# Transform mixing with a squared-ReLU layer on one core: the order of VectorE's sums, its side work and ScalarE's side work inside a step

## The chip, the core and the metric

The kernel runs on one core of a Trainium2 chip. PE is TensorE (matmuls; PEld its weight loads), DVE VectorE, ACT ScalarE, POOL GpSimd, and SP the engine that issues most DMAs. Every engine works its own instructions strictly in the order in which the program lists them, and waits on semaphores for the others. SBUF is the on-chip memory, PSUM the accumulators into which PE writes, in banks. The metric is the device time of one execution in microseconds (us); every time below is in us.

## The reference

```python
X = np.fft.fft(x, axis=1); X = np.fft.fft(X, axis=2)   # x: (8, 3008, 256) float32
a = X.real.reshape(8 * 3008, 256)
h = a @ w_in                                           # w_in: (256, 2048)
r = np.maximum(h, 0.0)
out = (r * r) @ w_out                                  # w_out: (2048, 256)
```

Eight batches, each a real part of a two-dimensional Fourier transform, then two matrix products with a squared ReLU between them, all in float32.

## The kernel before

**Blocks and steps.** A batch has 1506 columns (the transform's symmetry gives the rest), cut into six blocks of 252 columns (`CK`; the last has 246). The 2048 hidden features are 16 chunks of 128, taken in pairs, so a block has `NJ` = 8 steps, and the program 384, numbered `i`. "Step 2" below means i modulo 8 = 2. The loop at the end of the function lists one step's instructions for all engines; since each engine keeps that order, the place of a call in the loop is its place in the engine's queue.

A step's *front* (`front`, L928 to L935): four PE products of 252 columns, two into the bank hP and two into hQ; then DVE's *split*: two operations on hP (L932, tile `he`) and two on hQ (L934, L935), each writing one half of the hidden tile g and, mirrored, the other. Then ACT's relu (L939) and square (L942) on g, and POOL's sums of thirds of g (`sums_even`, L955 to L957, in even steps, `sums_odd`, L965 to L972, in odd ones) into a tile s.

Behind the front, in the same step, PE runs the *back* of an earlier pair of steps: the second matrix product, as a fast product of small matrices with 20 instead of 24 block products. In odd steps `first_half` runs 12 products from g and s into the banks F0, F1, F2, in even steps `second_half` 8 products from s into S0, S1, S2 (L990; each bank holds three slots of 168 columns). Their weights are sums of parts of w_out, kept in `wsum` (12 of them) and in place, which `sum_wout` (L379) makes on DVE beside steps 8 to 14 of batch 0.

**The gather.** After four pairs a block's banks are full. `gather` returns five functions that bring them together in the tile c: `early` (two ACT copies out of F1 and F2, L1045 and L1046), `upper` (two DVE operations that read F0, L1049 and L1050), `lower` (an ACT copy out of S0 and six DVE operations, L1053 to L1059, that read S0, S1, S2), `joins` (L1062 to L1065; L1064 still reads S0) and `rest` (L1068 to L1070). A block's last first half falls into step 1 of the next block, `early` at its end; `upper` into step 2, `lower` behind that step's second half, `joins` into step 3, `rest` into step 4. `store` (DVE transposes at L1105 and L1107, eight DMAs from SP) follows for the two mirror halves in steps 5 and 6; in the last block it goes over PE transposes (L1089). The next block's first half needs the F banks in step 3, its second half the S banks in step 4.

**The next batch's transform.** `ahead(b + 1)` is a list of pieces, each a planned time and a function, that prepare the next batch beside the steps of this one. First come DVE's folds of the eight tiles of x (`fold`: fs at L520, fd at L524, which also issues the load three tiles ahead, sc at L536, dc at L540, w at L550, a shuffle at L560) and rotations between them (butterflies at L573 and L574, turns at L596 and L625); pieces of planned time 0.0 between these are ACT's (copies and scalings, L583 to L631, tables L410 to L417). For batch 1 there are also small pieces for one separate column (L464 to L494) and four transform groups for it. Last come eight transform groups (`even` and `odd`, the functions in the set `beside`): eight small PE products each into a bank `pd`, ACT copies (L688, L766, L791) and DVE joins (L711 to L717, L799 to L819). The pool `psh` has two banks in turn for hP, hQ and pd, so a group takes hP's bank once the split has read it, and the next step's hQ takes pd's once the joins have read that.

`SHARE` and `pace` spread the planned times over a batch's steps: each step may spend pace x share. `pieces_beside(False)` runs right behind the front and lists pieces while the budget and a step's room (1.9, in batch 0 2.4) last, those of time 0.0 at once. `pieces_beside(True)` is called by `run` before the fourth product of a half (the hook) and lists a transform group.

The order in a step is: front, pieces, then `upper`, `joins` or `rest` when due (`pending`), then `store` when due, the first or second half with its hook, `lower`, relu, square, POOL's sums, `early`.

Of the kernel before, what the change touches and what calls it, by code (L numbers as in the profile page):

```python
# [9 lines left out]
F32 = mybir.dt.float32  # L10
# [5 lines left out]
P = 128  # L16
# [68 lines left out]
def kernel(  # L85
# [12 lines left out]
    nc = tc.nc  # L98
# [7 lines left out]
    NJ = NFC // 2  # L106
# [29 lines left out]
    tt = nc.vector.tensor_tensor  # L136
    act = nc.scalar.activation
# [235 lines left out]
    def place(to):  # L373
        return wsum[:, to] if isinstance(to, int) else to

    def sum_wout(qs, which):

        u, v, op, to = SUMS[which]
        tt(out=place(to)[:, qs], in0=u[:, qs], in1=v[:, qs], op=op)  # L379
# [568 lines left out]
    gt = nc.gpsimd.tensor_tensor  # L948
# [45 lines left out]
    def first_half(q, n, gA, gB, s, hook=None):  # L994

        if q == 0:
            open_banks(("F0", "F1", "F2"))
        a, b = thirds(gA, n), thirds(gB, n)
        r1, r3, r0, r2 = ([v[:, h] for v in w] for w in (a, b) for h in range(2))
        run((("F0", 2, 0, r2[2]), ("F0", 1, 1, r2[1]), ("F0", 1, 2, s[:, 9]), ("F0", 0, (1, 2), r2[0]),  # L1000
             ("F0", 0, 3, s[:, 0]), ("F1", 2, (1, 1), r1[2]), ("F2", 1, (0, 0), r0[0]), ("F2", 1, 9, s[:, 1]),
             ("F2", 0, (0, 3), r3[2]), ("F1", 0, 6, r0[2]), ("F1", 1, 5, r3[1]), ("F1", 1, 4, s[:, 11])), q, n, hook)

    def second_half(q, n, s, hook=None):

        if q == 0:
            open_banks(("S0", "S1", "S2"))
        run((("S0", 0, 8, s[:, 2]), ("S0", 1, (0, 1), s[:, 4]), ("S0", 2, (0, 2), s[:, 8]), ("S1", 0, (1, 0), s[:, 6]),
             ("S1", 1, 11, s[:, 10]), ("S1", 2, 10, s[:, 3]), ("S2", 0, 7, s[:, 7]), ("S2", 1, (1, 3), s[:, 5])),
            q, n, hook)  # L1010
# [21 lines left out]
    def gather(n):  # L1032
# [3 lines left out]
        cf = ep.tile([P, 5, TB], F32, name="cf", tag="cf")[:, :, 0:tb]  # L1036
        cs = ep.tile([P, 2, TB], F32, name="cs", tag="cs")[:, :, 0:tb]
        vt = ep.tile([P, 7, TB], F32, name="vt", tag="vt")[:, :, 0:tb]
# [3 lines left out]
        u4 = cf[:, 4]  # L1042

        def early():
            nc.scalar.copy(cf[:, 2:5], F1)  # L1045
            nc.scalar.copy(cf[:, 0:2], F2[:, 0:2])  # L1046

        def upper():
            tt(out=o1[0], in0=F0[:, 0], in1=u4, op=SUB)  # L1049
            tt(out=pair(1, 1), in0=F0[:, 1:3], in1=cf[:, 4:5].to_broadcast([P, 2, tb]), op=ADD)  # L1050

        def lower():
            nc.scalar.copy(cs, S0[:, 0:2])  # L1053
            tt(out=o1[0], in0=o1[0], in1=S0[:, 0], op=SUB)
            tt(out=o1[2], in0=o1[2], in1=S0[:, 2], op=ADD)
            tt(out=cf[:, 3], in0=cf[:, 3], in1=S0[:, 1], op=SUB)
            tt(out=vt[:, 0:2], in0=S1[:, 0:2], in1=cs, op=ADD)
            tt(out=vt[:, 3:5], in0=S2[:, 0:2], in1=vt[:, 0:2], op=ADD)
            tt(out=vt[:, 2], in0=S1[:, 2], in1=vt[:, 4], op=ADD)  # L1059

        def joins():
            tt(out=vt[:, 5:7], in0=cf[:, 0:3:2], in1=vt[:, 2:4], op=ADD)  # L1062
            tt(out=o0[2], in0=vt[:, 6], in1=vt[:, 5], op=SUB)
            tt(out=o0[2], in0=o0[2], in1=S0[:, 2], op=ADD)  # L1064
            tt(out=pair(0, 0), in0=cf[:, 1:4:2], in1=vt[:, 5:7], op=ADD)  # L1065

        def rest():
            tt(out=pair(1, 1), in0=pair(1, 1), in1=vt[:, 0:4:3], op=ADD)  # L1068
            tt(out=pair(1, 1), in0=pair(1, 1), in1=vt[:, 1:3], op=SUB)  # L1069
            tt(out=o1[0], in0=o1[0], in1=vt[:, 4], op=ADD)  # L1070
# [202 lines left out]
    SHARE = (1.2, 1.2, 0.6, 0.0, 0.6, 0.8, 0.8, 1.2)  # L1273

    def share(i):
        return 0.0 if i < PLAIN + 2 else SHARE[i % NJ]

    def pieces_beside(at_hook):


        nonlocal spent
        room = 1.9 if i >= per else 2.4
        while side:
            t, f = side[0]
            if f in beside:
                if at_hook and spent + t / 2 <= 0:
                    side.pop(0)
                    f()
                    spent += t
                return  # L1290
            if t and (at_hook or t > room or spent + t / 2 > 0):
                return
            side.pop(0)
            f()
            spent, room = spent + t, room - t

# [113 lines left out]
    i = 0  # L1410
# [4 lines left out]
    for i in range(PLAIN, len(steps) + 7):  # L1415
# [15 lines left out]
        hook = None  # L1431
        if PLAIN <= i < len(steps):
            spent -= pace * share(i)
            pieces_beside(False)
            hook = (3, lambda: pieces_beside(True))
        while pending and pending[0][0] <= i:
            pending.pop(0)[1]()
        while finished and finished[0][0] <= i:
            store(*finished.pop(0)[1:])
        group = (i - 3) // 2  # L1440
# [4 lines left out]
        elif at >= NJ and at < len(steps):  # L1445
            b_, k0_, n_, j_ = steps[at]
            q = j_ // 2
            if not last_half:
                first_half(q, n_, made["g", at], made["g", at + 1], made["s", group], hook)
                if q == NJ // 2 - 1:  # L1450
                    c_, ops = gather(n_)
                    gather_next = ops[0]
                    final = at + 2 == len(steps)
                    pending += [(i + 1, ops[1]), (i + 2, ops[3]), (i + 3, ops[4])]
                    lower = (i + 1, ops[2])
                    finished += [(i + 3 + final * k + (not final) * (1 + k), b_, k0_, n_, s_, c_, final)
# [9 lines left out]
        if gather_next:  # L1466
            gather_next()

# [62 lines left out]
```

## Time and profile before

| what | value |
|---|---|
| median of 3 runs | 1994.09 us (1993.31 to 1999.09) |
| profiled execution | 1996.1 us |
| its span, first to last instruction | 1994.3 us |
| mean granted TensorE clock | 0.988 |
| busy: PE, DVE, POOL, ACT | 1899.8, 1722.7, 1564.0, 966.6 us |
| DVE waits for PE's hP (he L932) | 149.8 us in 101 waits |
| POOL waits for ACT (s L965 behind g L942) | 261.9 us in 150 waits |
| PE waits for DVE's second upper operation (F behind c L1050) | 17.7 us in 12 waits |

The profile is one execution. A row of a group gives the line, the engine, output and inputs, and the mean duration; a row of waits gives the waiting instruction, what it waited for, the total, the number of times and the longest. Rows of the timeline are start, length, engine, line and tiles, with the wait in brackets. Rows of stretches give the busy time of each engine between two times and the clock that TensorE was granted (1.00 is full). Neighbouring DVE rows overlap a little, so a row's duration is somewhat more than an instruction's share of DVE's time.

### The profile page before, as it was taken

The numbers are of one execution on the slowest core, as the hardware profiler recorded it, in microseconds if no ns is written. First come the engines' busy times: TensorE is split into PE (matmuls) and PEld (weight loads), VectorE is DVE, ScalarE is ACT, GpSimd is POOL, SyncE is SP. The second block draws the span as 40 slices with busy tenths as digits, with TensorE's granted clock in tenths as the row PEclk, the third lists the DMA queues.
The fourth block names the chain that finished last, engine by engine and source line by source line (L and its number), as shares of the span: only waits on it lengthen the run. The fifth ranks groups of instructions, "written<-read, shape, count | busy, mean of one in ns | idle before, by whom it ended". The sixth has DMA issues, their size and how long they took to land. (4 is left out here: it accounts for less than half of the span.)

```text
span 1994.3 us, 33439 instructions
## 1 busy us (share of the span) xinstructions
PE 1899.8 (95%) x11408; PEld 1765.2 (89%) x11408; DVE 1722.7 (86%) x3462; ACT 966.6 (48%) x1274; POOL 1564.0 (78%) x2111
## 2 busy tenths in 40 slices
PE   9989889999999989999999999999999999999998
PEld 7678889898898989989898998989989998999997
DVE  8798988999889998999879998899978999766765
ACT  5744444455444454445444544445544455444443
POOL 3477767898788877888778887788877888688886
PEclk9998999999999999999999999999999999999999
DMA  6331101111011101111101120111101110010010
GB/s 196 101 42 22 46 14 30 38 42 22 14 39 41 37 16 22 40 37 34 23 22 29 38 43 14 22 37 40 33 14 30 40 25 14 14 25 16 14 24 22
DMA packets 151306, 68.43 MB, mean 34 GB/s; under 512 B 131143, under 2 KB 142881, under 8 KB 151136
## 3 DMA queue, kind: packets, MB, share of 16 engines
q1 hardware_dynamic: 150590, 65.74, 15.0%
q8 instruction: 91, 1.49, 0.3%
q14 instruction: 79, 0.65, 0.1%
q0 software_dynamic: 416, 0.43, 0.1%
q10 hardware_dynamic: 130, 0.12, 0.0%
HBM read 41.54 MB, written 24.69 MB: 33 GB/s over the span
## 5 line engine op out<-in xcount | busy, mean ns | idle before, releaser
L939 ACT ACTIVATE g<-g 128x1008 f32<-128x1008 f32 (+1 forms) x384 | 399.8, 1041 | 684.6 <-DVE g L935 541.1
L932 DVE SCALAR_TENSOR_TENSOR he<-ew,gE,hP 128x252 f32<-128x252 f32 (+1 forms) x748 | 317.4, 464 | 150.9 <-PE hP L928 149.8
L928 PE MATMUL hQ<-Qt,G 128*128 128x252 f32 (+3 forms) x1496 | 385.3, 380 | 36.2 <-DVE dc L717 13.4
L942 ACT ACTIVATE g<-g 128x1008 f32<-128x1008 f32 (+1 forms) x384 | 399.4, 1040 | 12.0
L928 PE MATMUL hP<-Pt,G 128*128 128x252 f32 (+1 forms) x1496 | 379.3, 376 | 6.7 <-DVE he L932 6.7
L928 PEld LDWEIGHTS hQ<-Qt,G 128*128 128x128 f32 (+1 forms) x1496 | 277.3, 190 | 92.4 <-PE hP L928 28.5
L990 PE MATMUL F<-s,wsum 128*128 128x168 f32 (+1 forms) x1504 | 343.1, 310 | 0.0
L965 POOL TENSOR_TENSOR s<-g 128x168 f32<-128x168 f32 (+1 forms) x188 | 105.8, 563 | 268.3 <-ACT g L942 261.9
L990 PE MATMUL F<-g,wout 128*128 128x168 f32 (+1 forms) x1504 | 314.5, 312 | 0.0
L990 PE MATMUL F<-g,wsum 128*128 128x168 f32 (+1 forms) x1504 | 280.8, 310 | 17.7 <-DVE c L1050 17.7
L934 DVE TENSOR_TENSOR g<-he,hQ 128x504 f32<-128x504 f32 (+1 forms) x374 | 253.4, 678 | 49.9 <-DVE he L932 4.4
L928 PEld LDWEIGHTS hP<-Pt,G 128*128 128x128 f32 x1496 | 265.7, 190 | 26.8 <-DVE he L932 9.5
L990 PE MATMUL S<-s,wout 128*128 128x168 f32 (+1 forms) x1504 | 282.3, 306 | 0.1
L990 PE MATMUL S<-s,wsum 128*128 128x168 f32 (+1 forms) x1504 | 277.0, 307 | 4.7 <-DVE c L1064 3.3
L990 PEld LDWEIGHTS F<-g,wsum 128*128 128x128 f32 x1504 | 243.6, 193 | 30.9 <-issue 17.0
L990 PEld LDWEIGHTS S<-s,wsum 128*128 128x128 f32 x1504 | 238.1, 190 | 20.1 <-POOL s L957 5.4
L990 PEld LDWEIGHTS F<-s,wsum 128*128 128x128 f32 x1504 | 255.6, 194 | 0.0
L935 DVE TENSOR_TENSOR g<-he,hQ 128x504 f32<-128x504 f32 (+1 forms) x374 | 250.5, 670 | 0.0
L990 PEld LDWEIGHTS F<-g,wout 128*128 128x128 f32 x1504 | 247.7, 195 | 0.5 <-issue 0.5
L990 PEld LDWEIGHTS S<-s,wout 128*128 128x128 f32 x1504 | 232.2, 190 | 0.7 <-POOL s L972 0.4
L968 POOL TENSOR_TENSOR s<-s 128x336 f32<-128x336 f32 (+1 forms) x188 | 184.0, 979 | 14.7
L955 POOL TENSOR_TENSOR s<-g 128x336 f32<-128x336 f32 (+1 forms) x188 | 174.6, 929 | 23.4 <-ACT g L942 18.8
(210 smaller groups left out, 2720.1 us busy)
## 6 DMA issues: line engine op xcount, KB each, us to landing
out_dram<-os SPq DMA_DIRECT2D x376, 56.0 KB
xt<-in_x_dram SPq DMA_DIRECT2D x39, 384.0 KB
xt<-in_x_dram SPq DMA_DIRECT2D x63, 128.0 KB
ew<-e_dram SPq DMA_DIRECT2D x39, 126.0 KB
out_dram<-os SPq DMA_DIRECT2D x288, 7.0 KB
raw<-in_moe_w_in_dram SPq DMA_DIRECT2D x16, 256.0 KB
raw<-in_moe_w_out_dram SPq DMA_DIRECT2D x16, 256.0 KB
xt<-in_x_dram SPq DMA_DIRECT2D x2, 512.0 KB
```

The lines of the kernel that those rows point to most:

```text
L928: nc.tensor.matmul(to[:, h, 0:n], w[:, fs], v[:, ks], start=h == 0, stop=True, skip_group_check=True)
L932: nc.vector.scalar_tensor_tensor(out=t[:, h, 0:n], in0=window[b, k0][:, 0:n], scalar=gE[:, fc:fc + 1], in1=hP[:, h, 0:n], op0=ALU.mult, op ...
L934: tt(out=g[:, :, 0:n], in0=t[:, :, 0:n], in1=hQ[:, :, 0:n], op=ALU.add)
L935: tt(out=g[:, :, n:2 * n][:, :, ::-1], in0=t[:, :, 0:n], in1=hQ[:, :, 0:n], op=ALU.subtract)
L939: act(g[:, :, 0:2 * n], g[:, :, 0:2 * n], AF.Relu)
L942: act(g[:, :, 0:2 * n], g[:, :, 0:2 * n], AF.Square)
L955: gt(out=s[:, 0:2], in0=a0, in1=a2, op=ADD)
L965: gt(out=s[:, 11], in0=b2[:, 0], in1=b1[:, 0], op=SUB)
L968: gt(out=s[:, 4:6], in0=s[:, 4:6], in1=s[:, 10:11].to_broadcast([P, 2, tb]), op=SUB)
L990: nc.tensor.matmul(acc[nm][:, slot, 0:tb], w, v, start=q == 0 and nm not in begun, stop=q == NJ // 2 - 1, skip_group_check=True)
```

## The change

- `gather`: `early` copies three slots instead of five. `upper` has three more DVE operations that read F1 and F2 from PSUM and form the upper results in c. `lower` adds S0's third slot to both halves at once, so that nothing behind it reads S0. `joins` is three operations and `rest` three of 168 columns, without PSUM. `rest` is listed in step 5; in the last block it goes to POOL, inside `lower`.
- The order in a step: front, `pending`, `store`, then the pieces, then the half. The pieces of time 0.0 are no longer listed among the others but at the end of the step (`free_pieces`), behind relu, square, POOL's sums and `early`; a piece of 0.0 at the head of the list ends a step's pieces.
- `SHARE` has 0.0 in steps 2 and 3 and 1.6 in steps 1 and 7; batch 0 has shares of its own (`FIRST`) and a room of 3.0. The hook stands before the third product.
- `store` falls into steps 6 and 8 (step 0 of the block after).
- In `first_half` two slots of F1 change places, in `second_half` S1's third product comes last.
- Six of the 32 weight sums go to POOL (three in each of steps 8 and 9).

```diff
     def sum_wout(qs, which):
-        tt(out=place(to)[:, qs], in0=u[:, qs], in1=v[:, qs], op=op)
+        (gt if which % 2 and qs.start == 0 and which < 12 else tt)(out=place(to)[:, qs], in0=u[:, qs], in1=v[:, qs], op=op)
...
-             ("S1", 1, 11, s[:, 10]), ("S1", 2, 10, s[:, 3]), ("S2", 0, 7, s[:, 7]), ("S2", 1, (1, 3), s[:, 5])),
+             ("S1", 1, 11, s[:, 10]), ("S2", 0, 7, s[:, 7]), ("S2", 1, (1, 3), s[:, 5]), ("S1", 2, 10, s[:, 3])),
...
         def early():
-            nc.scalar.copy(cf[:, 2:5], F1)
-            nc.scalar.copy(cf[:, 0:2], F2[:, 0:2])
+            nc.scalar.copy(cf[:, 1:3], F1[:, 0:2])
+            nc.scalar.copy(cf[:, 0], F2[:, 0])
 
         def upper():
-            tt(out=o1[0], in0=F0[:, 0], in1=u4, op=SUB)
-            tt(out=pair(1, 1), in0=F0[:, 1:3], in1=cf[:, 4:5].to_broadcast([P, 2, tb]), op=ADD)
+            tt(out=o1[0], in0=F0[:, 0], in1=cf[:, 2], op=SUB)
+            tt(out=pair(1, 1), in0=F0[:, 1:3], in1=wide(cf[:, 2:3]), op=ADD)
+            tt(out=o0[1], in0=F1[:, 2], in1=cf[:, 1], op=ADD)
+            tt(out=o0[2], in0=F1[:, 0], in1=cf[:, 0], op=SUB)
+            tt(out=o0[0], in0=F2[:, 1], in1=cf[:, 0], op=ADD)
 
         def lower():
             nc.scalar.copy(cs, S0[:, 0:2])
             tt(out=o1[0], in0=o1[0], in1=S0[:, 0], op=SUB)
-            tt(out=o1[2], in0=o1[2], in1=S0[:, 2], op=ADD)
-            tt(out=cf[:, 3], in0=cf[:, 3], in1=S0[:, 1], op=SUB)
+            tt(out=o0[1], in0=o0[1], in1=S0[:, 1], op=SUB)
+            tt(out=both, in0=both, in1=wide(S0[:, 2:3]), op=ADD)
             tt(out=vt[:, 0:2], in0=S1[:, 0:2], in1=cs, op=ADD)
             tt(out=vt[:, 3:5], in0=S2[:, 0:2], in1=vt[:, 0:2], op=ADD)
-            tt(out=vt[:, 2], in0=S1[:, 2], in1=vt[:, 4], op=ADD)
+            if final:
+                rest()
+            tt(out=v13, in0=S1[:, 2], in1=v14, op=ADD)
 
         def joins():
-            tt(out=vt[:, 5:7], in0=cf[:, 0:3:2], in1=vt[:, 2:4], op=ADD)
-            tt(out=o0[2], in0=vt[:, 6], in1=vt[:, 5], op=SUB)
-            tt(out=o0[2], in0=o0[2], in1=S0[:, 2], op=ADD)
-            tt(out=pair(0, 0), in0=cf[:, 1:4:2], in1=vt[:, 5:7], op=ADD)
+            tt(out=pair(0, 0), in0=pair(0, 0), in1=vt[:, 2:4], op=ADD)
+            tt(out=v13, in0=v8, in1=v13, op=SUB)
+            tt(out=both, in0=both, in1=wide(vt[:, 2:3]), op=ADD)
 
         def rest():
-            tt(out=pair(1, 1), in0=pair(1, 1), in1=vt[:, 0:4:3], op=ADD)
-            tt(out=pair(1, 1), in0=pair(1, 1), in1=vt[:, 1:3], op=SUB)
-            tt(out=o1[0], in0=o1[0], in1=vt[:, 4], op=ADD)
+            late(out=v9, in0=v9, in1=v15, op=SUB)
+            late(out=o1[1], in0=o1[1], in1=v9, op=ADD)
+            late(out=o1[0], in0=o1[0], in1=v14, op=ADD)
...
-    SHARE = (1.2, 1.2, 0.6, 0.0, 0.6, 0.8, 0.8, 1.2)
+    SHARE = (0.5, 1.6, 0.0, 0.0, 0.5, 0.6, 0.5, 1.6)
+    FIRST = (1.2, 1.6, 0.3, 0.5, 1.0, 1.0, 1.0, 1.6)
 
     def share(i):
-        return 0.0 if i < PLAIN + 2 else SHARE[i % NJ]
+        return 0.0 if i < PLAIN + 2 else FIRST[i % NJ] if i < per else SHARE[i % NJ]
+
+    def free_pieces():
+        while side and not side[0][0]:
+            side.pop(0)[1]()
+
+    def pieces():
+        nonlocal spent
+        room = 1.9 if i >= per else 3.0
+        while side:
+            t, f = side[0]
+            if f in beside or not t or t > room or spent + t / 2 > 0:
+                return
+            side.pop(0)
+            f()
+            spent, room = spent + t, room - t
+
+    def piece_beside():
+        nonlocal spent
+        if side and side[0][1] in beside and spent + side[0][0] / 2 <= 0:
+            t, f = side.pop(0)
+            f()
+            spent += t
...
-        hook = None
-        if PLAIN <= i < len(steps):
-            spent -= pace * share(i)
-            pieces_beside(False)
-            hook = (3, lambda: pieces_beside(True))
         while pending and pending[0][0] <= i:
             pending.pop(0)[1]()
         while finished and finished[0][0] <= i:
             store(*finished.pop(0)[1:])
+        hook = None
+        if i < len(steps) and share(i):
+            spent -= pace * share(i)
+            pieces()
+            hook = (2, piece_beside)
...
-                    pending += [(i + 1, ops[1]), (i + 2, ops[3]), (i + 3, ops[4])]
+                    pending += [(i + 1, ops[1]), (i + 2, ops[3])] + ([] if final else [(i + 4, ops[4])])
...
         if gather_next:
             gather_next()
+        free_pieces()
```

## The prediction

> **What bounds the kernel now.** I read the busy totals first, then the granted clock, then one batch cut into its six blocks beside two blocks of the last batch, which has no transform to prepare, then PE's waits in batches 1 to 6, then the instructions around two of these waits. "Step 2" is the step whose number modulo 8 is 2; a block has steps 0 to 7.
>
> ```profile
> PE 1899.8 (95%) x11408; PEld 1765.2 (89%) x11408; DVE 1722.7 (86%) x3462; ACT 966.6 (48%) x1274; POOL 1564.0 (78%) x2111
> ```
> ```profile
> core 0: 1994.3 us, clock 0.988
> ```
> ```profile
> 559.50:596.11 36.61, 36.57 (x227) 34.58 (x226) 34.21 (x64) 16.53 (x19) 31.12 (x42) 1.00 0.13 34
> 596.11:635.88 39.77, 37.63 (x226) 34.37 (x225) 38.55 (x69) 19.02 (x23) 33.18 (x45) 1.00 0.17 39
> 635.88:674.35 38.47, 37.44 (x227) 34.50 (x226) 37.08 (x72) 19.49 (x25) 34.66 (x46) 1.00 0.16 38
> 674.35:712.86 38.51, 37.38 (x226) 34.66 (x225) 36.85 (x68) 19.27 (x24) 33.46 (x44) 1.00 0.17 38
> 712.86:757.68 44.82, 40.46 (x258) 38.38 (x257) 39.29 (x84) 22.86 (x34) 33.85 (x48) 1.00 0.12 21
> 757.68:798.37 40.69, 39.65 (x258) 38.13 (x257) 31.09 (x69) 18.00 (x24) 30.71 (x44) 1.00 0.08 14
> ...
> 1798.10:1834.50 36.40, 36.40 (x226) 34.96 (x226) 24.85 (x51) 17.94 (x20) 30.89 (x46) 1.00 0.10 19
> ```
> ```profile
> PE hQ L928 <- DVE dc L717: 13.4, 6, 2.2
> PE F L990 <- DVE c L1050: 12.9, 10, 2.0
> PE hQ L928 <- DVE Pt L717: 10.5, 6, 2.1
> PE pd L787 <- DVE he L932: 6.2, 6, 1.0
> ```
> ```profile
> 609.90 1.62 DVE L596 SCALAR_TENSOR_TENSOR w<-w,turn,f 94x257 f32<-94x257 f32 x2
> 611.45 1.38 DVE L520 TENSOR_TENSOR fs<-xt 96x512 f32<-96x512 f32 x1
> 612.75 0.32 DVE L1049 TENSOR_TENSOR c<-F,cf 128x168 f32<-128x168 f32 x1
> 612.99 0.49 DVE L1050 TENSOR_TENSOR c<-F,cf 128x336 f32<-128x336 f32 x1
> 613.63 0.81 PE L990 MATMUL F<-g,wsum 128*128 128x168 f32 x4 [2.00 <-DVE c L1050]
> ```
> ```profile
> 727.30 1.01 DVE L574 TENSOR_TENSOR w<-f,w 94x257 f32<-94x257 f32 x1
> 728.25 0.32 DVE L1049 TENSOR_TENSOR c<-F,cf 128x168 f32<-128x168 f32 x1
> 729.61 0.34 DVE L717 TENSOR_TENSOR dc<-db,pd 128x188 f32<-128x188 f32 x1
> 730.10 1.09 PE L928 MATMUL hQ<-Qt,G 128*128 128x252 f32 x4 [2.24 <-DVE dc L717]
> ```
>
> In the stretches the columns are length, then busy time of PE, PEld, DVE, ACT, POOL. In the last batch a block is pure PE: 36.40 of 36.40, with DVE at 24.85. A block of 246 columns is then 36.4 x 246/252 = 35.5, and a transform group costs PE 0.87 (eight records from 724.52 to 725.39), so a batch with eight groups can't be under 5 x 36.4 + 35.5 + 7.0 = 224.5. Batch 2 takes 238.9, 14.4 over: 0.2, 3.4, 2.1, 2.1, 4.9, 1.7 by block. In blocks 1 to 3 DVE is busy 37 to 38.6, more than PE's 36.4, so DVE sets them. In block 4 it is order: pieces stand ahead of the sums that free F (the wait at 613.63) and of the joins that free a transform's bank, which the next hQ takes (730.10).
>
> **Counting DVE's lateness.** A split takes DVE 2.15 back to back and unhindered ends 3.06 after its front starts. Steps are 5.12 (odd) and 3.98 (even). The next hQ starts 0.85 into the next step, so PE waits once a split is late by more than 2.9 (odd) or 1.8 (even). Lateness grows by 2.15 plus other DVE work less the step. Costs are mean rows less the 0.08 by which neighbours overlap: fs 1.0, fd 0.93, sc 0.72, dc 0.68, w 1.5 (two of 0.82), a shuffle 0.64, a butterfly 1.6, a pair of turns 1.36. For the old order, with its waits for F and for transform banks, this gives 0, 1.7, 2.4, 1.2, 5.2, 0.9 by block: 11.4 against the trace's 14.4, short mainly in block 1.
>
> **The change, part by part.**
>
> *The sums.* Old: upper 0.65, lower 2.1, joins 1.74, rest 2.3 = 6.8. New: upper has three more reads of PSUM at 0.24 (the spacing of L1054 to L1056) = 1.37; lower trades a 168-wide for a 336-wide one, +0.17 = 2.27; joins of two 336- and one 168-wide operations 1.65; rest of three 168-wide ones on SBUF, 0.36 (shortest L1063) to 0.73 each (mean L1070), taken at 0.57 = 1.7. That is 7.0: DVE's load doesn't fall. ACT's two copies lose 0.2. F's first two operations come where they came, F1 and F2 are used five products (1.43) later, so the longer upper is hidden there.
>
> *Pieces behind the sums, new shares.* I wrote the pieces out by plan: their sum is 48.6 per batch, and the pace rises from 1.34 to 1.64 a share. Steps 2 and 3 get none. For example block 2 has fd, sc, dc in step 0, w and shuffle in 1, fs and fd in 4, sc, butterfly, dc in 5 (behind rest: 4.7 in all), w in 6, turns and shuffle in 7. Its lateness runs 2.4, 3.0, 2.1, 3.6, 1.6, 1.7, 3.4, 2.1, and the waits past 2.9 and 1.8 sum to 3.3. In the same way the blocks give 0, 0.6, 3.3, 2.4, 3.0, 0.9 = 10.2. Of block 4's 3.0, 2.4 is new: the first transform group stands in step 5 behind step 4's two last butterflies (3.2), its bank is hP's, and hP is freed 2.4 late for a group that now stands behind two products, 0.29 earlier than behind three. Differences to the old count: -1.1, +0.9, +1.2, -2.2 in blocks 1 to 4, -1.2 together; and the wait for F, counted at 1.2, is 2.0 in the trace and leaves whole, so I take -2.3 a batch, -14 for six. Ends: -43, if the four waits above go (13.4 + 12.9 + 10.5 + 6.2) and nothing follows; +13, if those come back and blocks 2 and 3 lose their 2.1.
>
> *The clock.* The mean grant of 0.988 costs 0.012 x 1994 = 24. It drops for 3.4 at a time, 1.7 lost, seven times in batches 1 to 6 (0.64 granted from 1700.5 to 1705.2, behind a 2.11 idle), always behind idle of 2.0 or more, though not behind each. Three such idles per batch become one: -8 of 12; ends -12 and 0. The Trainium skill (TensorE: Matmul & The Clock Gate, Part 1) has the clock fall after a whole idle window of about 3.4 us. The trace disagrees: 2.0 us were enough. By that page this term would be nothing and the time 8 us longer.
>
> *Batch 0.* Four steps hold 22.5 over their floor of 5.12 (and 0.87 for a group): 10.10 at 145.7, 13.22 at 169.0, 9.65 at 239.3, 11.79 at 264.0. At 169.0 the table copies and the first group share a step, with DVE 2.3 late; the new plan has the copies at that step's end and the group a step later: -5.7. At 264.0 the last butterflies still stand ahead of the joins, but hP's 3.8 wait goes: -3.3. At the other two, pieces still follow: -1 and -1.3. The wait for S behind L1064 (2.2, once) goes, as lower frees S: -1.5. Sum -12.8; ends -18 and -5.
>
> *Six weight sums to POOL.* Alone they are 0.34 apart on DVE (three in 1.09 at 90.35), with POOL busy 0.76 is common and 1.12 the longest. Between -2 (six gone) and +2 (the other six stretched to the longest, two taken off): 0, as POOL waits there (4.55 before 92.73) and PE waits for DVE by no more than 0.4 before 111. The Trainium skill (SBUF — State Buffer, Who interferes with whom) says that a DVE instruction with two SBUF inputs and a GpSimd instruction that reads SBUF exclude each other. By that rule six pairs follow one another, 6 x (0.34 + some 0.7, between POOL's 0.54 for 168 and 0.89 for 336) = 6.2 for the old 4.1, and the sum would be 2 higher.
>
> *At nothing.* ACT's pieces behind the squares: PE's waits for POOL are 1.1 in six batches though POOL waits 185.8 for ACT, and the next relu waits for a split behind the pieces anyway; uncovered, POOL's sums come late to the S products, up to the 1.6 of one turn. Stores move from steps 5 and 6 to 6 and 8, ahead of the pieces: eight issues of some 0.4 on SP now stand before a step's xt load, which leads by three tiles; DVE waited 2.5 for xt once, at the start. The load of POOL in the blocks is unchanged. The order of products within F and S changes no count.
>
> *The end.* Rest leaves DVE for POOL there, but upper is 0.7 longer ahead of lower, with PE's 4.0 wait behind it all: -0.5 (-1.5 to +0.5).
>
> Sum: -14 - 8 - 12.8 - 0.5 = -35. The profiled execution took 1996.1 (span 1994.3 and 1.8 around), 2.0 over the median of the runs: 1996.1 - 35 - 2 = **1959**.
>
> **The rivals.** (1) The waits go and little returns, since collisions with POOL thin out: -43 - 12 - 18 - 1 = -74, 1920, or half way, 1938. For: blocks 0 and 5 have DVE room (34.2 and 31.1). Against: 1 to 3 have none. (2) The order changes but DVE's bound holds: the waits of blocks 1 and 4 return as late splits, +13, against -12.8 in batch 0: 1994, no change. For: DVE's 38.55 in a 39.77 block. Against: block 4's waits are order, not load. (3) Slower: pieces bunched behind odd steps collide with POOL. L550 takes 0.34 to 1.17 by where POOL stands; squares that come earlier keep POOL busy through more pieces. Priced by the count, pieces 10% dearer bring 15.6 a batch against the old 11.4, +25, and no clock gain: 1994 + 25 - 13 = 2006. It decides from about 5%. For: DVE rows with two SBUF inputs scatter, those with PSUM don't. Against: three rests of 168 replace 336s. By the Trainium skill's rule above, whichever starts second stands for the other's whole instruction.
>
> **How the numbers follow.** Forecast 0.64 (own range 1940 to 1980, from -2.3 a batch give or take 3); rival 1 0.14, rival 2 0.09, rival 3 0.13. Faster by over 0.3%, about what the measurement can tell: 0.64 + 0.14 = 0.78; same 0.09; slower 0.13. The range of 1932 to 1994 leaves out rival 3 and the lower part of rival 1.
>
> **What would show it.** Right: no PE wait for upper in F, nor of some 2 for a transform's joins in hQ; blocks 1 to 5 of a batch near 38, 39.4, 39.7, 41.7 and 41.5 (one group moves from block 4 to 5); the step at 169 under 9; a grant above 0.99. Wrong: DVE busy over 38 in each of blocks 1 to 3, longer L550 and L520 rows, PE waiting for he at the group of step 5 by more than 2.4, or for POOL in S.

## The result and the profile after

The changed kernel takes 1966.59 us (median of 4 runs, 1963.47 to 1970.06) beside 1993.7 for the kernel before (4 runs): ratio 0.9859, 95% interval 0.9834 to 0.9883, so 1.4% faster. The forecast was 1959, 1.8% faster. The profiled execution took 1965.07, 1.5 under the median.

The page's busy totals and the granted clock, after:

```profile
PE 1889.9 (96%) x11408; PEld 1764.7 (90%) x11408; DVE 1719.0 (88%) x3547; ACT 958.9 (49%) x1274; POOL 1549.7 (79%) x2120
```
```profile
core 0: 1963.3 us, clock 0.991
```

Batch 2 of the changed kernel, cut into its six blocks (length, then busy time of PE, PEld, DVE, ACT, POOL):

```profile
550.68:587.61 36.93, 36.55 (x227) 34.71 (x226) 33.94 (x65) 16.18 (x18) 31.88 (x43) 1.00 0.15 39
587.61:625.51 37.90, 37.14 (x226) 34.75 (x225) 36.74 (x69) 19.14 (x24) 32.42 (x45) 1.00 0.11 28
625.51:665.55 40.04, 37.63 (x227) 34.66 (x226) 38.84 (x74) 19.38 (x25) 33.71 (x46) 1.00 0.17 47
665.55:704.62 39.07, 37.15 (x227) 34.81 (x226) 37.88 (x72) 19.25 (x25) 32.97 (x44) 1.00 0.13 36
704.62:745.76 41.14, 39.35 (x251) 37.58 (x250) 36.38 (x83) 22.30 (x33) 31.28 (x45) 1.00 0.08 18
745.76:786.23 40.47, 40.47 (x267) 39.12 (x265) 33.05 (x75) 17.95 (x25) 31.21 (x44) 1.00 0.07 17
```

PE's waits in batches 1 to 6 (total, times, longest), after:

```profile
PE hP L929 <- DVE he L933: 18.7, 18, 1.4
PE hQ L929 <- DVE g L936: 11.2, 33, 0.4
PE pd L670 <- DVE he L933: 9.0, 6, 2.1
```

Three readings. The blocks with transform pieces, 1 to 5, were forecast near 38, 39.4, 39.7, 41.7 and 41.5, and are 37.90, 40.04, 39.07, 41.14 and 40.47: the gain of the batch sits in blocks 1 and 4 (39.77 and 44.82 before), and block 2 is 1.6 longer. In the mean of batches 1 to 6 it is much the same (block 1 37.6 for 40.4, block 4 41.1 for 45.6, block 2 40.05 for 38.4), but block 3 is longer by more than in batch 2: 39.9 for 37.8, of which 0.85 is clock. The four waits that made 43.0 of PE's idle time are all gone; DVE's late splits (he, g) have taken their place with 38.9. And by stretch, the fronts of the steps mark 321.8 us up to the end of batch 0 before and 313.9 after, 1436.3 and 1414.4 for batches 1 to 6, 236.2 and 235.0 for the rest: -7.9, -21.9 and -1.2, together the -31.0 between the two spans.

### The profile page after: what moved, and what is told of

The parts are those of the page before. It is cut to its first block, busy times and chain, and to the rows that moved or that the text cites. A ratio compares the mean times of both kernels' runs of the same rounds, so it can differ in the third digit from the quotient of the medians.

```text
span 1963.3 us, 33452 instructions
## 1 busy us (share of the span) xinstructions
PE 1889.9 (96%) x11408; PEld 1764.7 (90%) x11408; DVE 1719.0 (88%) x3547; ACT 958.9 (49%) x1274; POOL 1549.7 (79%) x2120
## 3 DMA queue, kind: packets, MB, share of 16 engines
q1 hardware_dynamic: 150590, 65.74, 13.4%
## 5 line engine op out<-in xcount | busy, mean ns | idle before, releaser
L990 PE MATMUL F<-g,wout 128*128 128x168 f32 (+1 forms) x1504 | 308.1, 307 | 0.0
L990 PE MATMUL S<-s,wsum 128*128 128x168 f32 (+1 forms) x1504 | 306.7, 306 | 0.0
L990 PEld LDWEIGHTS S<-s,wsum 128*128 128x128 f32 x1504 | 250.6, 191 | 8.4
L990 PEld LDWEIGHTS F<-s,wsum 128*128 128x128 f32 x1504 | 251.2, 192 | 0.3 <-issue 0.3
L990 PEld LDWEIGHTS F<-g,wout 128*128 128x128 f32 x1504 | 243.0, 192 | 0.0
L968 POOL TENSOR_TENSOR s<-s 128x336 f32<-128x336 f32 (+1 forms) x188 | 180.6, 961 | 14.7
L971 POOL TENSOR_TENSOR s<-s 128x336 f32<-128x336 f32 (+1 forms) x188 | 174.2, 927 | 14.7
```

What stands on the lines that cost most here:

```text
L968: gt(out=s[:, 4:6], in0=s[:, 4:6], in1=s[:, 10:11].to_broadcast([P, 2, tb]), op=SUB)
L971: gt(out=s[:, 6:9:2], in0=s[:, 2:4], in1=s[:, 6:8], op=ADD)
L990: nc.tensor.matmul(acc[nm][:, slot, 0:tb], w, v, start=q == 0 and nm not in begun, stop=q == NJ // 2 - 1, skip_group_check=True)
```

## The experiments

Each ratio is to the kernel before on the same chip, in five rounds; beside it stands the changed kernel's 0.9859. "Clock lost" is one less the grant, times the time, summed over a stretch of the record of the granted clock; a span of 3.41 at half clock loses 1.7. Lengths of steps run from the start of one front to that of the next.

### ScalarE's pieces ahead of relu again

```diff
+        free_pieces()
         if i < len(steps):
             relu(n, g)
             square(n, g)
             sums_of(i)
         if gather_next:
             gather_next()
-        free_pieces()
```

> The changed kernel with one thing put back: ScalarE's pieces of planned time 0.0 stand in each step ahead of relu again, everything on DVE, PE and POOL as changed. Theory (DVE's lateness and its order set the time, ScalarE's place costs nothing): 1967, within 4 either way; ACT waits for DVE's pieces ahead of relu again, POOL's waits for ACT grow, PE's waits stay what they are in the changed kernel. Rival (a later relu makes POOL's sums late, so ScalarE's place is a good part of the gain): 1978 or more, with PE waits for POOL in S.

Measured: 1986.93 us beside 1997.65, ratio 0.9951 [0.9938, 0.9963]. Two thirds of the gain are gone. Batches 1 to 6 take 1433.6 for 1414.4, and the clock lost in them is the same 6.8 in both kernels, though not in the same blocks. Block 4 is longer above all, 45.0 for 41.1 in the mean of the six batches: 1.2 of it in step 3, 0.7 in step 4, and 1.8 in step 5, where 0.9 is clock. Of PE's waits in batches 1 to 6, hP's for late splits fell from 18.7 to 6.9, but hQ's doubled (11.2 in 33 waits in the changed kernel), and a wait of F for upper came back:

```profile
PE hQ L929 <- DVE g L936: 22.5, 62, 0.7
PE F L990 <- DVE c L1053: 3.7, 6, 0.6
```

Here are the pieces of step 1 and the sums of step 2 of block 4 in batch 3, and the F of step 3 that waits for them. First the changed kernel's timeline (start, length, engine, line, tiles; the wait in brackets):

```profile
948.01 1.84 DVE L626 SCALAR_TENSOR_TENSOR w<-w,turn,f 94x128 f32<-94x128 f32 x4
...
948.18 1.04 ACT L940 ACTIVATE g<-g 128x1008 f32<-128x1008 f32 x1 [1.22 <-DVE g L936]
...
950.21 0.42 ACT L1048 COPY cf<-F 128x336 f32<-128x336 f32 x1
...
950.72 0.41 ACT L631 COPY f<-w 94x257 f32<-94x257 f32 x1
...
951.93 0.33 DVE L1052 TENSOR_TENSOR c<-F,cf 128x168 f32<-128x168 f32 x1
```

and the same stretch with the pieces ahead of relu:

```profile
955.82 3.09 DVE L626 SCALAR_TENSOR_TENSOR w<-w,turn,f 94x128 f32<-94x128 f32 x4
...
958.95 0.41 ACT L631 COPY f<-w 94x257 f32<-94x257 f32 x1 [2.16 <-DVE w L626]
...
959.57 1.04 ACT L940 ACTIVATE g<-g 128x1008 f32<-128x1008 f32 x1
...
961.59 0.42 ACT L1048 COPY cf<-F 128x336 f32<-128x336 f32 x1
...
962.04 0.33 DVE L1052 TENSOR_TENSOR c<-F,cf 128x168 f32<-128x168 f32 x1 [0.95 <-ACT cf L1048]
...
962.94 0.81 PE L990 MATMUL F<-g,wsum 128*128 128x168 f32 x4 [0.61 <-DVE c L1053]
```

The piece L631 needs DVE's turn L626, ACT waits 2.16 for it, and relu, square and the early copies stand behind. So upper waits 0.95 for an early copy, and F 0.61 for upper. POOL's sums, which start from the square, have moved against DVE's queue as well, and the four turns took 3.09 instead of 1.84. Over batches 1 to 6 the mean turn row is 725 ns here and 545 in the changed kernel. The turns alone don't make the loss: with the old shares, a faster kernel (below), their mean is 716.

### The early copies behind ScalarE's pieces

```diff
             sums_of(i)
+        free_pieces()
         if gather_next:
             gather_next()
-        free_pieces()
```

> The changed kernel with ScalarE's pieces between the sums and the early copies of a block's last first half: relu, square and GpSimd's sums stay ahead of them, the early copies go behind. Theory (the 4 to 5 us a batch that the pieces ahead of relu cost in block 4 come from the late relu and the late GpSimd sums, which then lie beside VectorE's pieces and gather): nothing of it returns here, ratio 0.984 to 0.988, like the changed kernel. Rival (they come from the early copies, which the upper of the next step waits for): ratio 0.991 to 0.996, the loss as with the pieces ahead of relu.

Measured: 1966.92 beside 1996.39, 0.9859 [0.984, 0.9878]. The early copies' place costs nothing as long as relu and square are ahead; what the run before lost hangs on relu, square and the sums that follow them, and on the early copies only as they stand behind these.

### ScalarE's place alone, in the old kernel

```diff
-            f()
+            if t or i < per:
+                f()
+            else:
+                behind.append(f)
...
         if gather_next:
             gather_next()
+        while behind:
+            behind.pop(0)()
```

> The kernel before with one part of the change: from batch 1 on, the pieces that ScalarE takes at a step's start run behind the step's relu, square, sums and early copies. Nothing else moves. Theory (what the run with ScalarE's pieces put ahead of relu lost, some 0.9%, is the price of that place in any order, because relu, square and GpSimd's sums wait behind a piece that itself waits for VectorE): ratio 0.990 to 0.997. Rival (the place only matters once VectorE's pieces run behind the upper and joins; in the old order ScalarE's piece has nothing of VectorE's to wait for at that point): ratio 0.998 to 1.003.

Measured: 1995.62 beside 1996.39, 0.9996 [0.9987, 1.0005]. The rival's range was right: the place is worth 0.9% in the new kernel and nothing in the old one. Of the old kernel's large waits three are little changed (hQ for joins 14.4 and F for upper 12.1 in batches 1 to 6, 13.4 and 12.9 before; pd for the split 6.2 in both), and hQ's other wait for joins fell from 10.5 to 7.7. The rival's reason, that ScalarE's piece has nothing to wait for there, was not shown.

### The order alone, in the old kernel

```diff
+        while pending and pending[0][0] <= i:
+            pending.pop(0)[1]()
+        while finished and finished[0][0] <= i:
+            store(*finished.pop(0)[1:])
         hook = None
         if PLAIN <= i < len(steps):
...
-        while pending and pending[0][0] <= i:
...
```

> The old kernel with one thing changed: sums due and stores are listed ahead of the pieces in each step. Theory: the waits for F behind upper (17.7 in all) go, but what they hid comes back as late splits, since blocks 1 to 3 are bound by DVE's load, and the waits of the transform groups stay: 1983 to 1994. Rival (the order in the step is the whole gain): 1972 or less.

Measured: 2004.88 beside 1997.65, 1.0048 [1.0034, 1.0062]: slower. Its waits in batches 1 to 6:

```profile
PE hQ L928 <- DVE dc L717: 18.7, 6, 3.1
PE hP L928 <- DVE he L932: 12.8, 18, 1.2
```

F's wait of 12.9 is gone, as the prediction said, but the splits' wait for hP has gone from 0.3 to 12.8, and the joins' from 13.4 to 18.7. What stood ahead of the sums now stands ahead of the next split. hQ's other wait for joins (Pt) went from 10.5 to 7.9.

### Order and ScalarE's place together, in the old kernel

The two diffs above in one kernel.

> The kernel before with two parts of the change, each of which alone gave nothing (order: ratio 1.005; ScalarE's place: 1.000): upper, joins, rest and stores ahead of the pieces, and from batch 1 on ScalarE's pieces at the step's end. Theory (the two need each other: with the sums ahead, a ScalarE piece ahead of relu waits for a VectorE piece that now stands later, and that is where the order lost): together they gain, 2 to 4 us a batch, ratio 0.987 to 0.994. Rival (the gain is made elsewhere, by rest in the odd step, the new hook and the old gather's end): ratio 1.000 to 1.006.

Measured: 2002.4 beside 1996.8, 1.0027 [1.0016, 1.0037]. They do not need each other; the theory fell. ScalarE's place is worth 0.2% beside the order in the old kernel (1.0048 to 1.0027, with intervals that just meet), not the 0.9% of the new one. The gain is made by something else, or by these two only beside other parts.

### The order undone in the new kernel

```diff
-        while pending and pending[0][0] <= i:
-            pending.pop(0)[1]()
-        while finished and finished[0][0] <= i:
-            store(*finished.pop(0)[1:])
         hook = None
         if i < len(steps) and share(i):
...
             hook = (2, piece_beside)
+        while pending and pending[0][0] <= i:
...
```

> The changed kernel with one part undone: the pieces stand ahead of upper, joins, rest and the stores again; ScalarE's pieces stay at the step's end. Theory (the prediction's: the waits of F for upper and of hQ and pd behind the joins come back, 2.3 us a batch and the clock's 8): 14 to 22 us of the gain go, ratio 0.992 to 0.998. Rival (the order of sums and pieces carries nothing by itself, as the kernel before with that order alone was slower by 0.5%): ratio 0.981 to 0.988.

Measured: 1967.07 beside 1996.8, 0.9853 [0.9838, 0.9867]: no change. Its waits in batches 1 to 6:

```profile
PE hP L929 <- DVE he L933: 22.2, 18, 1.6
PE hQ L929 <- DVE g L936: 11.4, 32, 0.4
PE pd L670 <- DVE he L933: 9.2, 6, 1.7
```

F's wait for upper and hQ's for the joins do not come back. The new shares are 0.0 in steps 2 and 3, where upper, lower and joins stand: with no pieces there, it makes no difference which of the two is listed first. Nor does a transform group stand there: the first one of a batch ran in step 2 of block 4, where hQ waited up to 2.2 for its joins, and now runs in step 5.

### Rest and the stores back a step

```diff
-                    pending += [(i + 1, ops[1]), (i + 2, ops[3])] + ([] if final else [(i + 4, ops[4])])
+                    pending += [(i + 1, ops[1]), (i + 2, ops[3])] + ([] if final else [(i + 3, ops[4])])
...
-                    finished += [(i + 3 + final * k + (not final) * (2 + 2 * k), b_, k0_, n_, s_, c_, final)
+                    finished += [(i + 3 + final * k + (not final) * (1 + k), b_, k0_, n_, s_, c_, final)
```

> The changed kernel with rest back in step 4 and the stores back in steps 5 and 6. Theory (rest's 1.7 us in an even step, whose split has 1.8 us to spare, make one more late split of up to 1 us a block in blocks 2 to 4, some 2 us a batch): ratio 0.989 to 0.994. Rival (step 4 has had few pieces since its share fell to 0.5, so rest fits there, and the stores are small): ratio 0.984 to 0.988, no change.

Measured: 1989.1 beside 1996.8, 0.9967 [0.9954, 0.998]. This undoes more than anything else. Batches 1 to 6 take 1433.7 for 1414.4. The loss is in step 5 of block 4 (12.1 for 8.1, means of batches 1 to 6), where the batch's first transform group stands, and in step 5 of block 5 (7.65 for 5.89); blocks 2 and 3 are shorter, by 0.8 and 1.9. Step 5 of block 4 in batch 3, the changed kernel:

```profile
961.39 1.14 DVE L574 TENSOR_TENSOR w<-f,w 94x257 f32<-94x257 f32 x1
...
964.88 0.46 DVE L933 SCALAR_TENSOR_TENSOR he<-ew,gE,hP 128x252 f32<-128x252 f32 x1
...
965.78 0.69 PE L670 MATMUL pd<-cosT,w 95*128 95x95 f32 x4 [1.77 <-DVE he L933]
...
967.02 0.34 DVE L1075 TENSOR_TENSOR vt<-vt 128x168 f32<-128x168 f32 x1
967.39 0.56 DVE L1076 TENSOR_TENSOR c<-c,vt 128x168 f32<-128x168 f32 x1
967.87 0.69 DVE L1077 TENSOR_TENSOR c<-c,vt 128x168 f32<-128x168 f32 x1
```

and with rest in step 4:

```profile
969.62 1.04 DVE L1075 TENSOR_TENSOR vt<-vt 128x168 f32<-128x168 f32 x1
970.70 0.94 DVE L1076 TENSOR_TENSOR c<-c,vt 128x168 f32<-128x168 f32 x1
971.56 0.67 DVE L1077 TENSOR_TENSOR c<-c,vt 128x168 f32<-128x168 f32 x1
972.15 0.78 DVE L574 TENSOR_TENSOR w<-f,w 94x257 f32<-94x257 f32 x1
...
975.64 0.47 DVE L933 SCALAR_TENSOR_TENSOR he<-ew,gE,hP 128x252 f32<-128x252 f32 x1
...
976.54 0.72 PE L670 MATMUL pd<-cosT,w 95*128 95x95 f32 x4 [4.16 <-DVE he L933]
```

with that step as a stretch (length, busy times, then the granted clock):

```profile
969.95:982.05 12.10, 7.94 (x42) 7.51 (x41) 9.30 (x19) 4.18 (x5) 7.92 (x12) 0.86 0.07 18
```

Rest takes 2.5 in front of the last two butterflies (four operations), the split behind them is later by about that, the group that takes hP's bank waits 4.16 instead of 1.77, and the clock falls behind it (0.86 granted in the step; in this step of all six batches, in the changed kernel of one). In step 5 of block 5 rest's three operations, 2.2 together, stand ahead of a group's joins, and hQ waits 1.5 for the bank. Rest and the stores were moved together; in neither of the two steps does a store stand ahead of the instruction that is waited for, so the loss there is rest's. The stores alone were not tried, nor was rest in step 5 of the old kernel.

### The old gather in the new order

```diff
-            nc.scalar.copy(cf[:, 1:3], F1[:, 0:2])
-            nc.scalar.copy(cf[:, 0], F2[:, 0])
+            nc.scalar.copy(cf[:, 2:5], F1)
+            nc.scalar.copy(cf[:, 0:2], F2[:, 0:2])
...
```

> The changed kernel with the old forms of the sums (early with five slots, upper 2, lower 6, joins 4 with S0's last reader, rest 3 of which two are 336 wide), in the changed order and steps; rest of the last block on DVE in its old step. Theory (DVE's load is 6.8 against 7.0 per block, 0.9 less in step 2, 0.6 more in step 5): waits after step 5 in blocks 2 and 3 grow by some 0.5 each, those in step 3 shrink by 0.5, so 1967 to 1973. Rival (the sums' new form, which frees S0 in step 2 and reads PSUM where POOL can't collide, is what gains): 1978 or more, with waits for S in step 4.

Measured: 1953.93 beside 1997.65, 0.9782 [0.9767, 0.9797]. In this run the old gather reads two slots of F1 that the new order of products has exchanged, so one part of the sum is formed of the wrong two slots; the work is the same. Upper, lower, joins and rest are the old ones too, with rest in step 5. The next run puts the slots back:

```diff
-             ("F0", 0, 3, s[:, 0]), ("F1", 1, (1, 1), r1[2]), ("F2", 1, (0, 0), r0[0]), ("F2", 1, 9, s[:, 1]),
-             ("F2", 0, (0, 3), r3[2]), ("F1", 0, 6, r0[2]), ("F1", 2, 5, r3[1]), ("F1", 2, 4, s[:, 11])), q, n, hook)
+             ("F0", 0, 3, s[:, 0]), ("F1", 2, (1, 1), r1[2]), ("F2", 1, (0, 0), r0[0]), ("F2", 1, 9, s[:, 1]),
+             ("F2", 0, (0, 3), r3[2]), ("F1", 0, 6, r0[2]), ("F1", 1, 5, r3[1]), ("F1", 1, 4, s[:, 11])), q, n, hook)
```

> The changed kernel with the old gather's forms and the old order of F1's slots, so that only the order of the pieces, the sums behind odd steps, ScalarE's place and the shares are new. Theory (the new gather's own instructions cost the 0.8% that the run with the old forms and the new slots showed; the slots' order in the first half is worth nothing by itself): ratio 0.976 to 0.981, the ops of the old gather at 43.8 us a batch against 46.8. Rival (it was the exchanged slots, not the forms, that shortened the blocks: F1's pair of slots closes earlier or later): ratio 0.984 or above, like the changed kernel.

Measured: 1953.74 beside 1996.39, 0.9787 [0.9773, 0.9801]. The slots are worth nothing, and the new gather costs 0.7% to 0.8%. Summed over batches 1 to 6 and divided by six, the gather's rows on DVE take 46.8 a batch in the changed kernel (17 rows a block), 43.8 here and 44.1 before (15 rows). Batches 1 to 6 are 11.4 shorter here, 3.4 of it clock.

### The old shares

```diff
-    SHARE = (0.5, 1.6, 0.0, 0.0, 0.5, 0.6, 0.5, 1.6)
+    SHARE = (1.2, 1.2, 0.6, 0.0, 0.6, 0.8, 0.8, 1.2)
```

> The changed kernel with the old shares of pieces in batches 1 to 6 (1.2, 1.2, 0.6, 0, 0.6, 0.8, 0.8, 1.2); batch 0 as changed. Theory by the count of lateness: waits of 0.6, 2.4, 0.4, 2.4, 4.7, 0.7 by block, 11.2 a batch against 10.2, so +6, and up to +8 for the clock, as three idles of over 2 stand in step 3 again: 1973 to 1981. Rival A (the order in the step is all): 1967. Rival B (the shares are all): 1985 or more.

Measured: 1957.85 beside 1997.65, 0.9806 [0.9792, 0.9819]: faster than the new shares by 0.5%, where the count had them slower. In batches 1 to 6:

```profile
PE hP L929 <- DVE he L933: 25.3, 19, 1.7
PE hQ L929 <- DVE g L936: 9.0, 26, 0.3
PE pd L670 <- DVE he L933: 1.8, 5, 0.4
```

The late splits, now in the steps behind step 2 with its 0.6, cost 6.6 more of hP, but the wait of the first transform group, here in step 4 of block 4 instead of step 5, falls from 9.0 to 1.8, and the clock lost from 6.8 to 3.4.

### Old gather and old shares together

> The same with the old shares in batches 1 to 6 as well. Theory (the two prices, 0.8% of the gather and 0.5% of the shares, stand apart: one is VectorE's load, the other where its pieces meet GpSimd): they add, ratio 0.971 to 0.976, 1941 to 1951 us beside a kernel before of 2000. Rival (both relieve the same lateness of VectorE in blocks 2 to 4, so the second finds nothing left to gain): ratio 0.977 to 0.982, no better than either alone.

Measured: 1942.41 us beside 1996.39, 0.973 [0.9717, 0.9743], the fastest kernel of the study: the two prices (0.8 and 0.5%) add to the 1.3% between it and the changed kernel. Batch 2:

```profile
545.90:582.16 36.26, 36.26 (x227) 34.71 (x226) 33.78 (x66) 16.24 (x18) 31.86 (x44) 1.00 0.18 42
582.16:620.64 38.48, 37.29 (x226) 34.74 (x225) 37.32 (x69) 19.77 (x25) 33.29 (x45) 1.00 0.16 38
620.64:657.72 37.08, 36.88 (x226) 34.73 (x225) 35.85 (x69) 19.33 (x25) 34.12 (x46) 1.00 0.18 40
```

Block 2 is 37.08 for 40.04. Batches 1 to 6 take 1395.0, and the record of the clock has no span at half in them (four in the changed kernel, seven before).

### Batch 0's shares as before

```diff
-    FIRST = (1.2, 1.6, 0.3, 0.5, 1.0, 1.0, 1.0, 1.6)
+    FIRST = (1.2, 1.2, 0.6, 0.1, 0.6, 0.8, 0.8, 1.2)
```

> The changed kernel with batch 0's shares as before, but 0.1 instead of 0.0 in step 3 (its room of 3.0 stays). Theory (the prediction's: of batch 0's gain the new plan carries the 5.7 at the old step at 169, where the copies and a group met): batch 0 ends 5 to 10 us later, ratio 0.988 to 0.991. Rival (batch 0 gained by the order and ScalarE's place, and a plan only moves the collisions to other steps): ratio 0.984 to 0.987.

Measured: 1963.39 beside 1996.8, 0.9837 [0.9824, 0.985]. Batch 0 ends at 313.9, to the tenth where it ends with the new plan, and the step that was 13.23 long at 169.0 is 5.12 with either. The rival was right.

## Why the prediction came out as it did

The total was near: 7.6 us, 0.4%, off the median, inside the forecast's own range. By stretch too: batches 1 to 6 were forecast at -22 (-14 and -8) and came to -21.9, of which 5.1 is clock (11.9 lost before, 6.8 after) and 16.8 the rest. But several terms were each wrong and cancelled, so that the closeness is in part luck. Undone one at a time in the new kernel, the place of rest and the stores is worth 1.1%, ScalarE's place 0.9%, and the order, the early copies' place and batch 0's shares nothing clear of the intervals (0.9853, 0.9859, 0.9837 for 0.9859); the new gather costs 0.7% to 0.8% and the new shares 0.5%.

**The sums.** "That is 7.0: DVE's load doesn't fall" priced the new gather at +0.2 a block and called it even. The rows give +0.45 (46.8 less 44.1, over six blocks); less the prediction's own 0.08 for each of two more rows, +0.29. Rest saves 0.32 instead of 0.6, joins 0.31 instead of 0.09. So the size was near; what failed is that no time was set against it. The runs give 0.7% to 0.8%, 13 to 15 us; the 11.4 in batches 1 to 6 are 0.32 a block, 0.09 of it clock. That this is DVE's time in blocks that DVE sets fits the sizes, but ACT's copies and the time at which S0 comes free changed with it.

**Pieces behind the sums.** Here the reason failed. The wait for F "leaves whole", and it did; but it was put down to the order, and beside the new shares the order carries nothing: undone in the new kernel it changes nothing (0.9853). Alone in the old one it is 0.5% slower, because what is moved ahead of the pieces moves the pieces towards the next split. Two parts of the change each remove F's wait, the shares that empty steps 2 and 3 (the run with the order undone) and the order (the run with the old shares); beside the one the other is idle for it. What the order is worth beside the old shares in the new kernel was not tried. hQ's waits for joins, 23.9 of the 43.0, stay under the order alone (26.6) and are gone in the new kernel with either the order or the shares undone; which other part removes them there stays open.

The block lengths came out within 1.1 of the forecast because the count saw the plan of the new kernel as a whole. Within that count sat the move of rest from the even step 4 to the odd step 5, never priced by itself; undone with the stores, it takes back 1.1 of the 1.4%. The count had the group of step 5 in block 4 right: PE idle 1.1 to 2.1 there, 2.4 forecast.

Some readings and sums under the count were off. The wait at 613.63, put down to block 4, lies in block 1 (596.11 to 635.88), as F's long waits do in all six batches, so that 2.0 of block 1's 3.4 was order, not load. A split's last row ends no sooner than 3.29 behind its front's start, where 3.06 was taken. PE does wait 1.35 for DVE at 89.20, just ahead of the first weight sum, so that "no more than 0.4 before 111" holds only from there on. And -1.2 and the 0.8 of F that the count lacked make -2.0 a batch, not -2.3.

**New shares.** By the count the old shares were worse in the new order, by 1.0 a batch; they are some 10 us better. Of the 8.4 between the two in batches 1 to 6, 3.4 is clock, which the count took to go the other way. Another 2.8 is in the waits shown (38.9 in 57 waits and 36.1 in 50), and seven waits fewer, if each leaves out the 0.24 that is measured for hQ (last section), are 1.7 by estimate. By block, old shares less new, the count had +0.6, +1.8, -2.9, 0, +1.7 and -0.2; measured are -0.3, +1.4, -2.4, -1.2, +1.3 and -0.3 a batch (a transform group's 0.87, which stands in block 4 instead of 5, taken out). So it went wrong in block 0, where the old shares cost nothing, and in block 3, where 0.6 of the 1.2 is clock.

**At nothing.** ACT's pieces behind the squares were called free, "the next relu waits for a split behind the pieces anyway", with 1.6 as the worst. Put back, they cost 0.9%, some 18 us. The cover doesn't hold in the new kernel: in the lines above ACT waits 2.16 for a turn, and relu stands behind it. The prediction looked for a price at PE's waits for POOL, which are 1.1; it is paid behind DVE, whose splits are late more often (hQ waits 22.5 for 11.2) and whose upper comes late (F waits 3.7). In the old kernel, where the same cover was read, the place is in fact worth nothing (0.9996).

**The clock.** The forecast was -8 of 12, and -5.1 was measured, within its ends. The grant is 0.991, over the 0.99 named.

**Batch 0.** The forecast was -12.8, and -7.9 was measured. The named steps did come: 13.23 to 5.12 at 169.0 (-8.1; forecast -5.7), 11.79 to 8.04 at 264.0 (-3.8; -3.3), 10.10 to 8.74 (-1.4; -1), 9.65 to 7.74 (-1.9; -1.3), the wait for S (-2.5; -1.5): -17.6. Steps that were not named gave 9.7 back, net: two steps with a moved group or a late split have 7.75 and 7.79 (6.07 and 5.12 before), the step behind the one at 145.7 runs at half clock (6.94 for 4.14), another has 6.13 for 3.98, and a step with a group's wait 10.13 for 8.07. And the plan was credited with the gain, which the run with the old shares refutes; 4.0 of the 7.9 go with the place of rest and the stores (batch 0 ends at 317.9 without it). Where the others come from stays open.

**The small ones.** The end gave -1.2 in span, 1.0 of it clock, for -0.5. The six weight sums on POOL, the new order of S1's products, the hook before the third product, the rule that a piece of 0.0 ends a step's pieces and batch 0's room of 3.0 were not tried alone.

**The rivals.** The first, waits gone and little returned, needed 1920 to 1938: the 43.0 went, but PE's other waits rose from 8.2 to 38.9, so no. The second, that DVE's load holds the time, is nearer than it was given credit for: blocks 2 and 3 are longer than before, and the old gather, with less DVE work, is what brings the next 0.8%. The third, that pieces collide with POOL, is seen where ScalarE's pieces stand ahead of relu and where rest stands in step 4; in the changed kernel the mean fs row fell (1.09 to 0.88) while sc (0.76 to 0.88) and fd (1.01 to 1.15) rose, and in batch 2 DVE was busy for over 38 in block 2 alone, so that it neither decided nor was absent. The range of 0.34 to 1.17 that was read for L550 is 0.41 to 1.14 in the rows of batches 1 to 6 before.

## What to carry to other kernels

When a change has several parts, price each by what it would do with the others left out and by what the others would do without it: here two parts did the same job on F's wait, and the one put first did nothing beside the other, while one called free takes back two thirds of the gain when it is undone. The order of two kinds of work in a queue matters only in steps that hold both, so look first at which steps hold both; then ask for each moved instruction what stands behind it, above all a split whose bank a matmul is waiting for. And an engine with time to spare, as ACT here at 49%, can still cost when it waits in front of something that others start from.

## What was not expected of the hardware

**The clock goes by fixed windows.** In the record of the granted clock all spans begin on one grid of 3.413 us. In the 14 profiles I cut the time by that grid and set PE's matmul time in each full-clock window against the clock of the next. Of 92 windows with PE busy for under 0.44, 91 were followed by half clock; from 0.44 to 0.55, 29 of 86; above 0.55, none of 7753. So the same wait costs 1.7 more or not, by where it falls. Two steps of the kernel before with the same wait of 2.1 show it, windows of the grid in batch 2:

```profile
738.65:742.07 3.42, 1.68 (x10) 1.24 (x9) 3.32 (x7) 1.71 (x2) 3.18 (x5) 1.00 0.00 0
742.07:745.48 3.41, 3.03 (x19) 2.97 (x20) 2.91 (x7) 0.60 (x1) 2.57 (x5) 1.00 0.00 0
```

and in batch 3:

```profile
977.59:981.00 3.41, 1.30 (x7) 0.87 (x6) 3.34 (x8) 0.95 (x1) 3.18 (x6) 1.00 0.00 0
981.00:984.41 3.41, 3.41 (x13) 3.16 (x12) 2.17 (x5) 0.85 (x1) 1.83 (x3) 0.50 0.00 0
```

In batch 2 the wait straddles two windows (1.68 and 3.03 busy; 1.68 is 0.49 of a window, where the clock may fall or not) and the clock stays at 1.00; in batch 3 it lies in one (1.30 busy), and the next is at 0.50. The Trainium skill (TensorE: Matmul & The Clock Gate, Part 1) has a free-running window of 3413 ns, and the grid agrees; it has the clock fall after an idle window, and here a window that was little more than half idle was enough.

**A wait of hQ costs 0.24 more than is seen.** In the 14 profiles I took the steps of batches 1 to 6 at full clock, in the blocks of 252 columns, without a transform group, whose one wait is ahead of hQ's first product. With a wait of 0.13 an even step lasts 4.35 (3.98 without); with 1.04 an odd one lasts 6.40 (5.12 without), with 2.24 it lasts 7.60. It is always the wait and 0.24 more, whatever its length. At 0.35 and 0.38, the commonest, up to another 0.1 comes on top (4.67 and 5.84): there hP's second product starts up to 0.31 behind its first, for 0.21 in a dense stream, which is too short an idle to be shown. Of the 0.24, some 0.17 is how the rows are made: a product's row, whose end is modelled, lasts 0.38, though the next starts after 0.21 in a dense stream, so that a wait counted from the end of the row leaves out the difference. The other 0.07 is hQ's second product, which starts 0.29 behind the first after a wait; why stays open. A sum of such waits from the profile is too low by 0.24 for each of them.

**DVE beside POOL.** Rest's three operations of 168 columns took 0.34, 0.56 and 0.69 in one place and 1.04, 0.94 and 0.67 in another; four turns took 1.84 and 3.09. All have two inputs in SBUF. Upper's first operation, also of 168 columns but with one input in PSUM, took 0.33 in both places above, with POOL's sums running beside it in both. The Trainium skill (SBUF — State Buffer, Who interferes with whom) has a DVE instruction with two SBUF inputs contend with a GpSimd instruction that reads SBUF, and one with a single SBUF input not; these rows agree. POOL's sums ran in both places of rest and of the turns too, so what makes one place dear and the other not, the rows don't show.
